# Hash-bucket attention and feed-forward in one kernel: work placed by step number instead of by generators, with reshaped hash loads

## Chip, cores, metric

The kernel runs on one core of a Trainium2 chip. The metric is the device time of one execution in microseconds (us). Kernels are compared through runs in the fast state, the quicker of two states.

The engines have short names here: PE does matmuls, ACT exps, DVE vector work, POOL copies and sums, and SP issues most of the DMA transfers. PSUM is the memory that matmuls write to.

## The reference, cut to what matters

```python
# q, k, v: (4, 8, 768, 64); proj: (64, 6); all float32
q_bits = (einsum('bhsd,dk->bhsk', q, proj) > 0)        # 6 sign bits per row, k likewise
mask   = q_bucket[:, :, :, None] == k_bucket[:, :, None, :]
scores = where(mask, scale * q @ k.T, -1e9)
attn   = softmax(scores) @ v
x      = attn.transpose(0, 2, 1, 3).reshape(B, S, 512)
xn     = (x - mean) / sqrt(var + 1e-6) * g_ln
out    = x + relu(xn @ w_ch1) @ w_ch2                  # 512 -> 2048 -> 512
```

Attention needs all heads of a batch before that batch's layer norm and feed-forward can start.

## The kernel before

Work is cut into 8 units (a batch and half its heads), each of 24 steps. A step is a pair (head, block of 128 keys): two score matmuls, one exp on ACT of 128x768, six attention matmuls. There are 192 steps; exp number n marks the start of step n in this text. A unit must be prepared before its first step: q and k are loaded twice (once by rows for the scores, once in 32-row chunks for the hash), the hash product is taken on PE in float32, its signs are appended to the rows, and the whole is transposed by DMA.

```python
def load_pair(ap, b, u):                      # issued at the start of a unit, for the next one
    hn = prep.tile([P, 4, NS * D], F32, tag="hashnat", bufs=2, name="hashnat")
    src = ap[b, hs].rearrange("h (c t s) d -> c h t (s d)", c=4, t=32)
    for c in range(4):
        nc.sync.dma_start(out=hn[:, c, :], in_=src[c])      # slowest source dim: 4 heads
    ...
# the main loop
for i in range(n_steps + LAG):
    ...scores(i); attend(i - LAG)
    if last step of batch b: ffq.append([i + FF_DELAY, b, feed_forward(b, layer_norm(b))])
    if i % 2 == 0: drain(nxt, 1)              # one more piece of the next unit's preparation
    credit = min(credit + 5.3, 8.0)           # feed-forward: up to 5.3 matmuls a step
    while ffq and ffq[0][0] <= i and credit >= 1.0: ...
# [cut: rest of the kernel]
```

A batch's feed-forward is 224 matmuls: 128 of 384 columns (first layer) and 96 of 512 (second). Relus are on DVE, as is the layer norm, emitted whole after the last head of a batch.

## Time and profile before

| | value |
|---|---|
| time, median of the first 3 runs | 512.64 us (508.14 to 519.0) |
| PE, DVE, ACT busy | 68%, 45%, 34% of the span |
| DMA queue of SP | 54.5% of 16 engines |
| exp 0 / 24 / 48 begin | 38.0 / 90.3 / 133.9 us |
| last exp begins / end of the span | 440.7 / 508.7 us |

The page's second part cuts the span in 40 slices; each digit is a busy share in tenths, and PEclk is the granted clock of PE in tenths. These rows are of the kernel before:

```profile
PE   0122339376926699689655896789368999909997
ACT  1001318254823145345612443446123555400000
PEclk9999855555558589899957999999677999968999
DMA  3965969759739334693469316934594110112101
```

PE does little for the first third. DMA is busier then, but the next view tells how. It is the busy time in stretches of 2 us (from, to, length; per engine busy time and count; then granted clock, DMA share, GB/s), kernel before:

```profile
12.00:14.00 2.00, 0.00 (x0) 0.00 (x0) 0.00 (x0) 0.00 (x0) 0.00 (x0) 1.00 0.27 100
...
46.00:48.00 2.00, 0.00 (x0) 0.00 (x0) 0.64 (x1) 0.00 (x0) 0.00 (x0) 1.00 0.27 99
...
76.00:78.00 2.00, 2.00 (x18) 1.28 (x17) 0.51 (x1) 1.86 (x3) 0.00 (x0) 0.50 0.98 406
```

Where hash loads run, the DMA share stands at about a quarter and 99 to 100 GB/s pass; where weights run, nearly all engines work and 406 GB/s pass. A share that stands still at a quarter says that 4 of 16 engines carry the transfer. That agrees with the Trainium skill, "DMA: Bandwidth & Descriptors", in the section on why a DMA adds 16 to its semaphore ("How many engines (k)"): the number of engines must divide the slowest dimension of both sides, and the source's slowest dimension is 4 heads.

The chain that ended last, in order of time (start, length, what), kernel before, shows such loads on the path in the middle too:

```profile
196.81 10.14 DMA hashnat<-in_k_dram
...
207.08 1.78 DVE hashT L116
...
211.33 1.51 PE hp L123 x16
```

A load issued at 196.81 us lands 10.14 us later, DVE transposes it, and the hash product follows on PE. Between 171 us and the last layer norm PE has six stops of over 2.5 us, of 3.2 to 8.3 us each.

### The profile page before, as it was taken

How to read it: one execution, taken by the hardware profiler on the slowest of the kernel's cores; microseconds unless marked ns; L12 is line 12 of the kernel's file. 1: busy time of each engine (PE TensorE's matmuls, PEld its weight loads, DVE VectorE, ACT ScalarE, POOL GpSimd, SP SyncE). 2: the span in 40 equal slices, each digit the busy share in tenths (PEclk: the TensorE clock that was granted, in tenths of full speed). 3: DMA queues.
4: the chain of work that ended last, by engine and by line, in shares of the span. 5: the costliest groups of instructions: out<-in, count | busy, mean ns of one | idle time of the engine just before them, and what ended most of it. 6: DMA issues, size and time to landing. Idle time of an engine off the chain costs nothing.

```text
span 508.7 us, 6653 instructions
## 1 busy us (share of the span) xinstructions
PE 344.2 (68%) x2696; PEld 191.4 (38%) x2696; DVE 229.6 (45%) x471; ACT 172.6 (34%) x193; POOL 67.5 (13%) x66
## 2 busy tenths in 40 slices
PE   0122339376926699689655896789368999909997
PEld 0011216243613255345423453455134556504453
DVE  0131054435492442463764424645744346385271
ACT  1001318254823145345612443446123555400000
POOL 3141140013110400150012201310104000000000
PEclk9999855555558589899957999999677999968999
DMA  3965969759739334693469316934594110112101
GB/s 102 187 149 141 294 166 283 258 152 170 151 89 178 80 63 109 187 140 84 132 146 191 70 51 185 193 71 118 122 195 107 40 41 1 43 26 59 41 22 62
DMA packets 90352, 62.31 MB, mean 122 GB/s; under 512 B 64209, under 2 KB 84689, under 8 KB 89809
## 3 DMA queue, kind: packets, MB, share of 16 engines
q1 hardware_dynamic: 90320, 61.88, 54.5%
q8 instruction: 21, 0.34, 0.3%
q14 instruction: 11, 0.08, 0.0%
HBM read 39.85 MB, written 6.29 MB: 91 GB/s over the span
## 4 chain that ended last, share of the span: by engine, by line
PE 37%; DMA 26%; DVE 21%; SPq 7%; issue 5%; POOL 2%; DVEq 0%; POOLq 0%
DMA hashnat<-in_q_dram 7%; PE sc L286 6%; DMA vnat<-in_v_dram 5%; SPq L99 4%; DMA hashnat<-in_k_dram 4%; DMA w1st<-in_moe_w_ch_dram 4%; PE av L303 3%; DVE hbuf L252 3%; DVE hashT L116 3%; DVE stats L200 3%; DMA scorenat<-in_k_dram 3%; DVE x L321 2%; PE hp L123 2%; DVE nd L315 2%; DVE xn L226 2%
## 5 line engine op out<-in xcount | busy, mean ns | idle before, releaser
L292 ACT ACTIVATE expb<-sc,bias_sb 128x768 bf16<-128x768 f32 x192 | 171.3, 902 | 268.0 <-PE sc L286 264.9
L286 PE MATMUL sc<-opT 70*128 70x384 bf16 x384 | 116.4, 392 | 4.9 <-DMA opT<-pad_86 1.7
L303 PEld LDWEIGHTS <-expb 128*128 128x128 bf16 x1152 | 73.5, 111 | 47.7 <-issue 30.5
L123 PE MATMUL hp<-hashT,projT 128*32 128x192 f32 x256 | 22.8, 503 | 88.2 <-DVE hashT L116 69.5
L247 PEld LDWEIGHTS <-w_sb 128*128 128x128 bf16 x512 | 48.6, 104 | 88.6 <-issue 56.2
L116 DVE STREAM_TRANSPOSE hashT<-hashnat 128x1536 f32<-128x1536 f32 x16 | 28.4, 1774 | 64.2 <-DMA hashnat<-in_k_dram 35.7
L286 PEld LDWEIGHTS <-opT 70*128 70x128 bf16 x384 | 37.9, 110 | 47.1 <-issue 27.2
L257 PEld LDWEIGHTS <-hbuf 128*128 128x128 bf16 x384 | 34.0, 97 | 32.4 <-issue 0.2
L123 PEld LDWEIGHTS hp<-hashT,projT 128*32 128x32 f32 x256 | 9.2, 153 | 94.3 <-DVE hashT L116 87.5
L303 PE MATMUL av<-vaug_92,expb 128*128 128x65 bf16 x432 | 30.0, 214 | 7.9 <-DVE nd L315 7.9
L303 PE MATMUL av<-vaug_91,expb 128*128 128x65 bf16 x432 | 29.5, 211 | 0.4 <-DVE nd L315 0.4
L315 DVE TENSOR_TENSOR nd<-av,vd 128x390 f32<-128x390 f32 x32 | 17.7, 553 | 23.4 <-PE av L303 23.4
L321 DVE TENSOR_TENSOR x<-nd,rec 128x384 f32<-128x384 f32 x32 | 21.9, 685 | 1.1
L112 POOL CAST pad_86<-scorenat 128x1536 bf16<-128x1536 f32 x5 | 7.5, 1490 | 110.4 <-DMA scorenat<-in_k_dram 69.4
L112 POOL CAST pad_85<-scorenat 128x1536 bf16<-128x1536 f32 x6 | 8.8, 1467 | 95.8 <-DMA scorenat<-in_k_dram 58.3
L112 POOL CAST pad_87<-scorenat 128x1536 bf16<-128x1536 f32 x5 | 7.3, 1468 | 106.1 <-DMA scorenat<-in_k_dram 78.7
L303 PE MATMUL av<-vaug_93,expb 128*128 128x65 bf16 x288 | 18.9, 207 | 0.0
L184 DVE TENSOR_SCALAR w_sb<-w1st,g_sb 128x2048 bf16<-128x2048 f32 x4 | 6.1, 1517 | 22.4 <-DMA w1st<-in_moe_w_ch_dram 22.4
L200 DVE BATCH_NORM_STATS2 stats<-x 128x6 f32<-128x512 f32 x24 | 16.0, 666 | 0.1
L226 DVE TENSOR_SCALAR xn<-x,mv,y 128x512 bf16<-128x512 f32 x24 | 11.3, 540 | 0.1
L247 PE MATMUL h_4072<-xT,w_sb 128*128 128x384 bf16 x4 | 1.5, 521 | 13.4 <-DMA xT<-xn 13.4
L189 DVE CAST w_sb<-w2st 128x2048 bf16<-128x2048 f32 x4 | 4.9, 1226 | 10.9 <-DMA w2st<-in_moe_w_ch_dram 10.9
(364 smaller groups left out, 401.1 us busy)
## 6 DMA issues: line engine op xcount, KB each, us to landing
hashnat<-in_k_dram SPq DMA_DIRECT2D x32, 192.0 KB
scorenat<-in_k_dram SPq DMA_DIRECT2D x8, 768.0 KB
hashnat<-in_q_dram SPq DMA_DIRECT2D x32, 192.0 KB
scorenat<-in_q_dram SPq DMA_DIRECT2D x8, 768.0 KB
vnat<-in_v_dram SPq DMA_DIRECT2D x8, 768.0 KB
out_dram<-res SPq DMA_DIRECT2D x24, 256.0 KB
w1st<-in_moe_w_ch_dram SPq DMA_DIRECT2D x4, 1024.0 KB
w2st<-in_moe_w_ch_dram SPq DMA_DIRECT2D x4, 1024.0 KB
```

What stands on the lines that cost most here:

```text
L112: nc.gpsimd.tensor_copy(pad[:, :, 0:D], sn.rearrange("p h (s d) -> p (h s) d", d=D))
L116: nc.vector.transpose(hT.rearrange("p c s j t -> p (c s j t)"), hn.rearrange("p c n -> p (c n)"))
L123: nc.tensor.matmul(hp[c * 32 : (c + 1) * 32, 0 : NS * 32], projT[:, j, :], hT[:, c, :, j, :], start=(j == 0), stop=(j == 1),)
L200: nc.vector.bn_stats(stats[:, s, :], x[:, s, :])
L226: nc.vector.tensor_scalar(xn[:, i, :], x[:, s, :], scalar1=mv[:, s, 0:1], scalar2=y[:, s : s + 1], op0=AOP.subtract, op1=AOP.mult,)
L247: nc.tensor.matmul(hp[:, 0:QH], w1_sb[:, o, n * P : (n + 1) * P], xT[hf][:, :, o, :], start=(o == 0), stop=(o == ND - 1),)
L257: nc.tensor.matmul(o2, hb[:, n, i * P : (i + 1) * P], w2_sb[:, n, :], start=(n == 0), stop=(n == NH - 1),)
L286: nc.tensor.matmul(sc[:, f, 0:QH], kT[0:KB, h * NS + t, :], qT[0:KB, h * NS + f * HALF : h * NS + (f + 1) * HALF, :],)
L292: nc.scalar.activation(e, sc[:, :, 0:QH], AF.Exp, scale=scale, bias=bias_sb)
L303: nc.tensor.matmul(av[:, s * VA : (s + 1) * VA], e[:, s // HALF, (s % HALF) * P : (s % HALF + 1) * P], va[:, h, t, :], start=(t == 0 and s ...
L315: nc.vector.tensor_add(nd, av[:, 0 : NS * VA].rearrange("p (s n) -> p s n", n=VA), vd[:, h : h + 1, :].to_broadcast([P, NS, VA]),)
L321: nc.vector.tensor_mul(xs[b][:, :, hd * D : (hd + 1) * D], nd[:, :, 0:D], rec.to_broadcast([P, NS, D]),)
```

## The change

The generators give way to a table from step number to actions. The stated intent: loads a unit ahead, stores and transposes issued late (when their data are ready), one hash transfer per head, the layer norm in pieces, and relus on two engines. The core of the diff, with cuts marked:

```diff
-        src = ap[b, hs].rearrange("h (c t s) d -> c h t (s d)", c=4, t=32)
-        for c in range(4):
-            nc.sync.dma_start(out=hn[:, c, :], in_=src[c])
+        src = ap[b, u * UH : (u + 1) * UH].rearrange("h (c t s) d -> h t c (s d)", c=4, t=32)
+        for h in range(UH):
+            eng.dma_start(out=hn[h * 32 : (h + 1) * 32], in_=src[h])
 ... (cut)
+    def plan_unit(n):
+        z = (n - 1) * UNIT
+        at(z + 0, cast_rows, n, "k")
+        at(z + 0, hash_turn, n, "k")
+        at(z + 3, hash_mm, n, "k")
+        at(z + 5, turn, n, "k")
 ...     (q likewise at 6, 6, 9, 11; v at 9 and 15)
+        if n + 1 < B * NU:
+            at(z + 3, load_hash, k, n + 1, "k", nc.sync)      # a unit ahead of its use
 ... (cut)
+                if n % 2:
+                    nc.scalar.activation(hb[:, n, :], hp[:, 0:QH], AF.Relu)
+                else:
+                    nc.vector.tensor_scalar_max(hb[:, n, :], hp[:, 0:QH], 0.0)
 ... (cut)
-                res = work.tile([P, DM], F32, tag="res", bufs=3, name="res")
-                nc.vector.tensor_add(res, o2, x[:, s, :])
-                nc.sync.dma_start(out=out_v[:, s, :], in_=res)
+                nc.vector.tensor_add(x[:, s, :], o2, x[:, s, :])
+                at(now[0] + 1, store, b, s)
 ... (cut: statistics of heads 0-3, 4-6 and 7 taken apart; x in 3 buffers, nd in 1)
+        first[b] = z + BATCH + FF_DELAY        # step 56, 104, 152, 200
+        if i < n_steps:
+            target = 0.0
+            for b in range(B):
+                left = TAIL_MM if b == B - 2 else 0                       # TAIL_MM = 45
+                span = BATCH if b < B - 2 else n_steps - first[b]
+                target += (N_FF - left) * min(max((i + 1 - first[b]) / span, 0.0), 1.0)
+        else:
+            target = done + 7
+        while ffq and done < target: ...
```

The first unit's q loads are also issued from ACT instead of SP, the tiny projection from the POOL queue, and the first unit is transposed in 4 parts.

More of the change, by code (lines that the diff above doesn't have):

```diff
@@ L69 @@
     for h in range(UH):
-        nc.sync.dma_start(
+        nc.gpsimd.dma_start(
             out=projT[h * 32 : (h + 1) * 32, :, h * NB : (h + 1) * NB], in_=proj_v
@@ L88, with at, run_step, load_hash @@
     w2ap = moe_w_ch2.rearrange("(o p) d -> p o d", p=P)
-    pad_no = [0]
+    todo = {}
+    def at(i, fn, *args):
+        todo.setdefault(i, deque()).append((fn, args))
+    def run_step(i):
+        for fn, args in todo.pop(i, ()):
+            fn(*args)
+    UNIT = UH * NS
     unit = {}
-    def load_pair(ap, b, u):
-        hs = slice(u * UH, (u + 1) * UH)
+    loaded = {}
+    half_done = {}
+    def load_hash(ap, n, key, eng):
+        b, u = divmod(n, NU)
         hn = prep.tile([P, 4, NS * D], F32, tag="hashnat", bufs=2, name="hashnat")
-        src = ap[b, hs].rearrange("h (c t s) d -> c h t (s d)", c=4, t=32)
-        for c in range(4):
-            nc.sync.dma_start(out=hn[:, c, :], in_=src[c])
+        src = ap[b, u * UH : (u + 1) * UH].rearrange("h (c t s) d -> h t c (s d)", c=4, t=32)
+        for h in range(UH):
+            eng.dma_start(out=hn[h * 32 : (h + 1) * 32], in_=src[h])
+        loaded[(n, key, "hash")] = hn
@@ L100, in load_pair, with load_rows @@
+    def load_rows(ap, n, key, eng):
+        b, u = divmod(n, NU)
         sn = prep.tile([P, UH, NS * D], F32, tag="scorenat", bufs=3, name="scorenat")
-        nc.sync.dma_start(
-            out=sn, in_=ap[b, hs].rearrange("h (p s) d -> p h (s d)", s=NS)
-        )
-        return hn, sn
-    def prep_side(ap, b, u, key):
-        hn, sn = load_pair(ap, b, u)
-        pad = pads[pad_no[0] % 3]
-        pad_no[0] += 1
-        yield
+        eng.dma_start(
+            out=sn,
+            in_=ap[b, u * UH : (u + 1) * UH].rearrange("h (p s) d -> p h (s d)", s=NS),
+        )
+        loaded[(n, key, "rows")] = sn
@@ L112, in prep_side, with pad_of, cast_rows, hash_turn @@
+    def pad_of(n, key):
+        return pads[(2 * n + (key == "q")) % 3]
+    def cast_rows(n, key):
+        sn = loaded.pop((n, key, "rows"))
         nc.gpsimd.tensor_copy(
-            pad[:, :, 0:D], sn.rearrange("p h (s d) -> p (h s) d", d=D)
+            pad_of(n, key)[:, :, 0:D], sn.rearrange("p h (s d) -> p (h s) d", d=D)
         )
+    def hash_turn(n, key):
+        hn = loaded.pop((n, key, "hash"))
         hT = prep.tile([P, 4, NS, 2, 32], F32, tag="hashT", bufs=1, name="hashT")
-        nc.vector.transpose(
-            hT.rearrange("p c s j t -> p (c s j t)"), hn.rearrange("p c n -> p (c n)")
-        )
@@ L119, in prep_side, with hash_mm @@
-        yield
+        for i in range(2):
+            nc.vector.transpose(
+                hT[:, 2 * i : 2 * i + 2].rearrange("p c s j t -> p (c s j t)"),
+                hn[:, 2 * i : 2 * i + 2].rearrange("p c n -> p (c n)"),
+            )
+        half_done[(n, key)] = hT
+    def hash_mm(n, key):
+        hT = half_done.pop((n, key))
         hp = ps_mm.tile([P, 512], F32, tag="mm", name="hp")
@@ L128, in prep_side @@
                 )
-        yield
         bits = prep.tile([P, NS, 32], F32, tag="bits", bufs=2, name="bits")
         nc.vector.transpose(bits.rearrange("p s n -> p (s n)"), hp[:, 0 : NS * 32])
-        dst = pad.rearrange("p (h s) n -> p h s n", s=NS)[:, :, :, D:KB]
+        dst = pad_of(n, key).rearrange("p (h s) n -> p h s n", s=NS)[:, :, :, D:KB]
         src = bits[:, :, 0 : UH * NB].rearrange("p s (h n) -> p h s n", n=NB)
@@ L138, in prep_side, with turn, value_cast, value_sum @@
             nc.vector.tensor_scalar_mul(dst, dst, 4.0 * BIG)
+    def turn(n, key, parts=1):
         tT = prep.tile([P, SL, P], BF16, tag="opT", bufs=4, name="opT")
-        nc.sync.dma_start_transpose(out=tT, in_=pad.rearrange("p a n -> p (a n)"))
-        unit[(b, u, key)] = tT
-        yield
-    def prep_v(b, u):
-        hs = slice(u * UH, (u + 1) * UH)
-        vn = prep.tile([P, UH, NS, D], F32, tag="scorenat", bufs=3, name="vnat")
-        nc.sync.dma_start(
-            out=vn.rearrange("p h s d -> p h (s d)"),
-            in_=v[b, hs].rearrange("h (p s) d -> p h (s d)", s=NS),
-        )
-        yield
-        va = vaugs[(b * NU + u) % 3]
+        w = SL // parts
+        for i in range(parts):
+            nc.sync.dma_start_transpose(
+                out=tT[:, i * w : (i + 1) * w, :],
+                in_=pad_of(n, key)[:, i * w : (i + 1) * w, :].rearrange("p a n -> p (a n)"),
+            )
+        unit[(n, key)] = tT
+    def value_cast(n):
+        vn = loaded.pop((n, "v", "rows")).rearrange("p h (s d) -> p h s d", d=D)
+        va = vaugs[n % 3]
         nc.gpsimd.tensor_copy(va[:, :, :, 0:D], vn)
-        v3 = prep.tile([P, UH, 3, D], F32, tag="v3", bufs=1, name="v3")
-        nc.gpsimd.tensor_add(v3, vn[:, :, 0:3, :], vn[:, :, 3:6, :])
         vs = prep.tile([P, UH, VA], BF16, tag="vs", bufs=1, name="vs")
         nc.gpsimd.memset(vs[:, :, D:VA], float(NS))
-        v1 = prep.tile([P, UH, D], F32, tag="v1", bufs=1, name="v1")
-        nc.gpsimd.tensor_add(v1, v3[:, :, 0, :], v3[:, :, 1, :])
-        nc.gpsimd.tensor_add(vs[:, :, 0:D], v1, v3[:, :, 2, :])
-        yield
+        nc.gpsimd.tensor_add(vn[:, :, 0:3, :], vn[:, :, 0:3, :], vn[:, :, 3:6, :])
+        nc.gpsimd.tensor_add(vn[:, :, 0, :], vn[:, :, 0, :], vn[:, :, 1, :])
+        nc.gpsimd.tensor_add(vs[:, :, 0:D], vn[:, :, 0, :], vn[:, :, 2, :])
+        half_done[(n, "v")] = (va, vs)
+    def value_sum(n):
+        va, vs = half_done.pop((n, "v"))
         vp = ps_mm.tile([P, 512], F32, tag="mm", name="vp")
@@ L165, in prep_v @@
         nc.vector.tensor_copy(vd.rearrange("p h n -> p (h n)"), vp[:, 0 : UH * VA])
-        unit[(b, u, "v")] = (va, vd)
-        yield
-    def prep_unit(b, u):
-        gens = [prep_side(k, b, u, "k"), prep_side(q, b, u, "q"), prep_v(b, u)]
-        for g in gens:
-            next(g)
-            yield
-        for g in gens:
-            for _ in g:
-                yield
-    def load_weights():
-        nc.sync.dma_start(out=g_sb, in_=moe_g_ln.rearrange("(o p) -> p o", p=P))
-        for o in range(ND):
-            st = work.tile([P, HID], F32, tag="hbuf", bufs=2, name="w1st")
-            nc.sync.dma_start(out=st, in_=w1ap[:, o, :])
-            yield
-            nc.vector.tensor_scalar_mul(w1_sb[:, o, :], st, g_sb[:, o : o + 1])
-        for o in range(4):
-            st = work.tile([P, 4, DM], F32, tag="hbuf", bufs=2, name="w2st")
-            nc.sync.dma_start(out=st, in_=w2ap[:, o * 4 : (o + 1) * 4, :])
-            yield
-            nc.vector.tensor_copy(w2_sb[:, o * 4 : (o + 1) * 4, :], st)
-        yield
@@ L193 @@
-    xs = {}
-    def layer_norm(b):
-        x = xs[b]
-        stats = work.tile([P, NS, 6], F32, tag="stats", bufs=2, name="stats")
+        unit[(n, "v")] = (va, vd)
+    def plan_unit(n):
[4 more added lines that the diff above has]
+        at(z + 5, turn, n, "k")
+        at(z + 6, cast_rows, n, "q")
+        at(z + 6, hash_turn, n, "q")
+        at(z + 9, hash_mm, n, "q")
+        at(z + 9, value_cast, n)
+        at(z + 11, turn, n, "q")
+        at(z + 15, value_sum, n)
+        if n + 1 < B * NU:
+            at(z + 3, load_hash, k, n + 1, "k", nc.sync)
+            at(z + 3, load_rows, k, n + 1, "k", nc.sync)
+            at(z + 9, load_hash, q, n + 1, "q", nc.sync)
+            at(z + 9, load_rows, q, n + 1, "q", nc.sync)
+            at(z + 15, load_rows, v, n + 1, "v", nc.sync)
@@ new lines, with load_w1, fold_w1, load_w2 @@
+    staged = {}
+    def load_w1(o):
+        st = work.tile([P, HID], F32, tag="hbuf", bufs=2, name="w1st")
+        nc.sync.dma_start(out=st, in_=w1ap[:, o, :])
+        staged[o] = st
+    def fold_w1(o):
+        nc.vector.tensor_scalar_mul(w1_sb[:, o, :], staged.pop(o), g_sb[:, o : o + 1])
+    def load_w2(o):
+        st = work.tile([P, 4, DM], F32, tag="hbuf", bufs=2, name="w2st")
+        nc.sync.dma_start(out=st, in_=w2ap[:, o * 4 : (o + 1) * 4, :])
+        staged[o] = st
+    def cast_w2(o):
+        nc.vector.tensor_copy(w2_sb[:, o * 4 : (o + 1) * 4, :], staged.pop(o))
@@ L198, in layer_norm, with stat, rstd @@
+    xs = {}
+    norm = {}
+    def stat(b, s, part, c0, c1):
+        if (s, part) == (0, 0):
+            norm[b] = work.tile([P, NS, 3, 6], F32, tag="stats", bufs=2, name="stats")
+        nc.vector.bn_stats(norm[b][:, s, part, :], xs[b][:, s, c0:c1])
+    def rstd(b):
+        stats = norm[b]
         mv = work.tile([P, NS, 2], F32, tag="mv", bufs=2, name="mv")
         for s in range(NS):
-            nc.vector.bn_stats(stats[:, s, :], x[:, s, :])
-            nc.vector.bn_aggr(mv[:, s, :], stats[:, s, :])
+            nc.vector.bn_stats(stats[:, s, 2, :], xs[b][:, s, DM - D : DM])
+        for s in range(NS):
+            nc.vector.bn_aggr(mv[:, s, :], stats[:, s, :, :].rearrange("p c n -> p (c n)"))
@@ L220, in layer_norm, with normalize, turn_x, store @@
             nc.vector.tensor_mul(y, y, t)
-        xT = []
-        for hf in range(2):
-            xn = work.tile([P, HALF, DM], BF16, tag="xn", bufs=2, name="xn")
-            for i in range(HALF):
-                s = hf * HALF + i
-                nc.vector.tensor_scalar(
-                    xn[:, i, :], x[:, s, :], scalar1=mv[:, s, 0:1],
-                    scalar2=y[:, s : s + 1], op0=AOP.subtract, op1=AOP.mult,
-                )
-            t_ = work.tile([P, HALF, ND, P], BF16, tag="xT", bufs=3, name="xT")
-            nc.sync.dma_start_transpose(
-                out=t_.rearrange("p s o n -> p (s o) n"),
-                in_=xn.rearrange("p s d -> p (s d)"),
-            )
-            xT.append(t_)
-        return xT
-    def feed_forward(b, xT):
-        x = xs[b]
-        out_v = out[b].rearrange("(p s) d -> p s d", s=NS)
-        for hf in range(2):
+        norm[b] = (mv, y)
+    xns = {}
+    def normalize(b, hf):
+        mv, y = norm[b]
+        xn = work.tile([P, HALF, DM], BF16, tag="xn", bufs=2, name="xn")
+        for i in range(HALF):
+            s = hf * HALF + i
+            nc.vector.tensor_scalar(
+                xn[:, i, :], xs[b][:, s, :], scalar1=mv[:, s, 0:1],
+                scalar2=y[:, s : s + 1], op0=AOP.subtract, op1=AOP.mult,
+            )
+        xns[(b, hf)] = xn
+    def turn_x(b, hf):
+        xn = xns.pop((b, hf))
+        t_ = work.tile([P, HALF, ND, P], BF16, tag="xT", bufs=3, name="xT")
+        nc.sync.dma_start_transpose(
+            out=t_.rearrange("p s o n -> p (s o) n"),
+            in_=xn.rearrange("p s d -> p (s d)"),
+        )
+        xns[(b, hf, "T")] = t_
+    now = [0]
+    def store(b, s):
+        out_v = out[b].rearrange("(p s) d -> p s d", s=NS)
+        nc.sync.dma_start(out=out_v[:, s, :], in_=xs[b][:, s, :])
+    def feed_forward(b):
+        x = xs[b]
+        for hf in range(2):
+            xT = xns.pop((b, hf, "T"))
             hb = work.tile([P, NH, QH], BF16, tag="hbuf", bufs=2, name="hbuf")
@@ L248, in feed_forward @@
                         hp[:, 0:QH], w1_sb[:, o, n * P : (n + 1) * P],
-                        xT[hf][:, :, o, :], start=(o == 0), stop=(o == ND - 1),
+                        xT[:, :, o, :], start=(o == 0), stop=(o == ND - 1),
                     )
-                    yield
-                nc.vector.tensor_scalar_max(hb[:, n, :], hp[:, 0:QH], 0.0)
+                    if o < ND - 1:
+                        yield
+                if n % 2:
+                    nc.scalar.activation(hb[:, n, :], hp[:, 0:QH], AF.Relu)
+                else:
+                    nc.vector.tensor_scalar_max(hb[:, n, :], hp[:, 0:QH], 0.0)
+                yield
             for i in range(HALF):
@@ L262, in feed_forward @@
                         yield
-                res = work.tile([P, DM], F32, tag="res", bufs=3, name="res")
-                nc.vector.tensor_add(res, o2, x[:, s, :])
-                nc.sync.dma_start(out=out_v[:, s, :], in_=res)
+                nc.vector.tensor_add(x[:, s, :], o2, x[:, s, :])
+                at(now[0] + 1, store, b, s)
                 yield
     LAG = 2
-    FF_DELAY = 8
+    FF_DELAY = 7
     N_FF = 2 * (NH * ND + HALF * NH)
+    BATCH = NU * UNIT
     steps = [
@@ L274 @@
     ]
-    UNIT = UH * NS
     exps = {}
     avs = {}
-    ffq = deque()
-    side = deque()
     def scores(i):
         b, u, h, t = steps[i]
-        qT, kT = unit[(b, u, "q")], unit[(b, u, "k")]
+        n = b * NU + u
+        qT, kT = unit[(n, "q")], unit[(n, "k")]
         sc = ps_sc.tile([P, 2, 512], F32, tag="sc", name="sc")
@@ L296, in attend @@
         b, u, h, t = steps[i]
-        va, vd = unit[(b, u, "v")]
+        va, vd = unit[(b * NU + u, "v")]
         if t == 0:
@@ L311, in attend @@
             if h == 0 and u == 0:
-                xs[b] = work.tile([P, NS, DM], F32, tag="x", bufs=2, name="x")
+                xs[b] = work.tile([P, NS, DM], F32, tag="x", bufs=3, name="x")
             hd = u * UH + h
-            nd = work.tile([P, NS, VA], F32, tag="nd", bufs=2, name="nd")
+            nd = work.tile([P, NS, VA], F32, tag="nd", bufs=1, name="nd")
             nc.vector.tensor_add(
@@ L324, in attend @@
             )
-    def drain(g, n=None):
-        c = 0
-        while n is None or c < n:
-            try:
-                next(g)
+    load_hash(k, 0, "k", nc.sync)
+    load_hash(q, 0, "q", nc.scalar)
+    load_rows(k, 0, "k", nc.sync)
+    load_rows(q, 0, "q", nc.scalar)
+    load_rows(v, 0, "v", nc.sync)
+    for key in ("k", "q"):
+        cast_rows(0, key)
+        hash_turn(0, key)
+        hash_mm(0, key)
+        if key == "k":
+            load_hash(k, 1, "k", nc.sync)
+        turn(0, key, UH)
@@ new lines @@
+    value_cast(0)
+    load_rows(k, 1, "k", nc.sync)
+    load_hash(q, 1, "q", nc.sync)
+    load_rows(q, 1, "q", nc.sync)
+    value_sum(0)
+    nc.sync.dma_start(out=g_sb, in_=moe_g_ln.rearrange("(o p) -> p o", p=P))
+    load_w1(0)
+    load_w1(1)
+    load_rows(v, 1, "v", nc.sync)
+    for n in range(1, B * NU):
+        plan_unit(n)
+    for o in range(4):
+        at(8 + 5 * o, fold_w1, o)
+        at(28 + 5 * o, cast_w2, o)
+        if o < 2:
+            at(8 + 5 * o, load_w1, o + 2)
+            at(28 + 5 * o, load_w2, o + 2)
+        else:
+            at(8 + 5 * o, load_w2, o - 2)
@@ new lines @@
+    first = {}
+    for b in range(B):
+        z = b * BATCH + LAG - 1
+        for s in range(NS):
+            at(z + UNIT + 2 * s, stat, b, s, 0, 0, UH * D)
+        for s in range(NS):
+            at(z + BATCH - NS + s, stat, b, s, 1, UH * D, DM - D)
+        at(z + BATCH, rstd, b)
+        at(z + BATCH, normalize, b, 0)
+        at(z + BATCH + 1, turn_x, b, 0)
+        at(z + BATCH + 1, normalize, b, 1)
+        at(z + BATCH + 3, turn_x, b, 1)
+        first[b] = z + BATCH + FF_DELAY
+    n_steps = len(steps)
@@ new lines @@
+    TAIL_MM = 45
+    ffq = deque()
+    done = 0
+    i = 0
+    while i < n_steps + LAG + FF_DELAY + 1 or ffq or any(j >= i for j in todo):
+        now[0] = i
+        if i < n_steps:
+            scores(i)
+        if LAG <= i < n_steps + LAG:
+            attend(i - LAG)
+        run_step(i)
+        for b in range(B):
+            if first[b] == i:
+                ffq.append(feed_forward(b))
+        if i < n_steps:
+            target = 0.0
+            for b in range(B):
+                left = TAIL_MM if b == B - 2 else 0
+                span = BATCH if b < B - 2 else n_steps - first[b]
+                target += (N_FF - left) * min(max((i + 1 - first[b]) / span, 0.0), 1.0)
+        else:
+            target = done + 7
+        while ffq and done < target:
+            try:
+                next(ffq[0])
+                done += 1
@@ L331, in drain @@
             except StopIteration:
-                return c
-            c += 1
-        return c
-    for _ in prep_unit(0, 0):
-        pass
-    nxt = prep_unit(0, 1)
-    drain(nxt, 3)
-    wts = load_weights()
-    credit = 0.0
-    n_steps = len(steps)
-    for i in range(n_steps + LAG):
-        if i < n_steps:
-            b, u, h, t = steps[i]
-            r = i % UNIT
-            if i and r == 0:
-                drain(nxt)
-                n = i // UNIT + 1
-                nxt = prep_unit(n // NU, n % NU) if n < B * NU else iter(())
-            scores(i)
-        if i >= LAG:
-            attend(i - LAG)
-            b, u, h, t = steps[i - LAG]
-            if (u, h, t) == (NU - 1, UH - 1, NS - 1):
-                ffq.append([i + FF_DELAY, b, feed_forward(b, layer_norm(b))])
-        if i < UNIT and i % 2 == 1:
-            drain(wts, 1)
-        if i % 2 == 0:
-            drain(nxt, 1)
-        credit = min(credit + 5.3, 8.0)
-        while ffq and ffq[0][0] <= i and credit >= 1.0:
-            if drain(ffq[0][2], 1) == 0:
@@ L364 @@
                 ffq.popleft()
-                continue
-            credit -= 1.0
-    while ffq:
-        drain(ffq.popleft()[2])
+        i += 1
 _INS = ['q', 'k', 'v', 'proj', 'moe_g_ln', 'moe_w_ch1', 'moe_w_ch2']
```

## The prediction

> **What bounds it now.** Nothing evenly; three stages. (Busy shares on the page: PE 68%, DVE 45%, ACT 34%; DMA 54.5% of 16 engines.)
>
> 1. 0 to 171 us, before any feed-forward: the load stream. First scores at 37.1 us (timeline), step 24 at 90, step 48 at 134 (counted exps), though a step needs ACT only 0.96 us. In stretches of 2 us the DMA share sits at exactly 0.27 with 99 GB/s wherever hash loads run (12-16, 26-28, 44-50, 104-110 us), while weights reach 341-406 GB/s. That is 4 of 16 engines. It agrees with the Trainium skill, "DMA: Bandwidth & Descriptors", section on the semaphore increment of 16, "How many engines (k)": k divides the slowest dim of both patterns, and the old source leads with 4 heads. The new pattern leads with 32 rows, so k should be 16. The old 786 KB takes about 7.9 us; I estimate 3.5-4 new.
> 2. 171 to 445 us: PE, broken by about one stop of 10-13 us per unit. The chain of waits shows load-issue, hash-load landing (10.1, 12.4, 10.2, 11.9 us), transpose 1.78, hash matmul. The loads are issued behind stores and transposes on SP, just before the in-order PE needs them. Layer norm also blocks DVE for about 12 us per batch.
> 3. 445 to 509 us: layer norm and transpose leave PE idle 13.4 us, then 50 us of feed-forward.
>
> **What changes.** Same matmuls and bytes. Loads come a unit (24 steps) ahead, so hash stops (about 12 us each) should vanish after start. Stores and transposes are issued when their data are ready, so SP no longer blocks (it waits 131.7 us at stores now). Half of the relus (0.56 us on DVE) go to ACT, estimated 0.55 us each there, 64 in all. One table load (1.28 us) should remain: "ScalarE: Activation LUTs", table sets, puts relu in every set; no trace of before tests it. Layer norm after the last head shrinks from about 11 to 7.5 us before the first transpose, and 45 matmuls (about 9 us) are held to cover it.
>
> **Sum (estimates from those durations).**
> - First scores at about 30 us instead of 37.
> - Steps 0-48 stay DMA-bound: loads of units 1, 2 and most of 3, 8.4 MB of weights (21 us), four transposes (3.75 each) make about 73 us, plus small gaps: step 48 at about 107.
> - First layer norm is not hidden (about 5 us of PE idle): feed-forward starts at about 121 instead of 171.
> - 136 steps with 627 feed-forward matmuls: at full clock a step's attention costs PE 0.44 us (1.325 us step less 5.3 matmuls of 0.163) and a feed-forward matmul 0.163 or 0.217: 60 + 117, plus ten hash products of 1.5, plus about 18 for PSUM waits on relu (DVE busy, ACT about 1.28 us a step in the first-layer phases, slightly over PE's 1.2): about 210 instead of 274.
> - Tail after the last step about 60 instead of 64.
>
> Predicted 392 us, 80% range 366 to 424. Chances: faster by over 2% 0.97, within 2% 0.02, slower 0.01.
>
> **Right or wrong shows as:** no long 0.27 DMA shares, hash loads near 200 GB/s; no PE wait over 3 us on the hash transpose after 121 us; PE busy 85-95% at clock near 1 from 121 us to the end; one table load; relu on ACT 0.5-0.6 us; PE idle in the final layer norm under 5 us instead of 13.4.
>
> **What would make it wrong:** hash loads into only 32 partitions at a time stay slow; transposes queued behind prefetched loads land late and scores wait at unit starts; weight folding on in-order DVE stalls attention in the first 48 steps; ACT's relus waiting on PE delay exps, making a PE-ACT lockstep; DVE (about 50 us of work per 63 us batch) becomes the limit.

## The result, and the profile after

The changed kernel takes 458.62 us (457.78 to 460.27, 4 runs), the kernel before 513.42 us. The ratio is 0.8967, with a 95% interval of 0.889 to 0.9044. Here and below, a ratio is from fast runs of the same rounds; it is not quite the ratio of the medians quoted, which are over all runs. The direction was right. The gain was 55 us where 121 was expected, and the time lies 35 us above the upper end of the range. All outputs are right.

The same rows of the changed kernel's page (40 slices of 11.4 us each):

```profile
PE   0476247936499998856899998864999988449996
ACT  1065144844230329966112169952303199503020
PEclk9998555785799999996699999977999999759999
DMA  8999999995493017990961068965110130030101
```

The first third is denser on DMA, as hoped. But look at ACT and PE together after the first third: where PE is at 9, ACT is mostly at 0 to 3; where ACT is at 9, PE is at 8. Attention and feed-forward alternate. In the kernel before, ACT stood mostly at 3 to 6 under a busy PE.

Busy time of two stretches of the changed kernel (columns as before: PE, weight loads, DVE, ACT, POOL, clock, DMA share, GB/s):

```profile
123.00:169.00 46.00, 45.76 (x240) 22.74 (x244) 13.64 (x24) 8.32 (x17) 2.93 (x2) 0.97 0.44 115
169.00:205.00 36.00, 27.86 (x359) 18.13 (x352) 21.90 (x46) 30.92 (x40) 7.92 (x7) 0.99 0.96 201
```

In the first stretch PE runs 240 matmuls, a whole feed-forward, and almost no attention. In the second ACT is busy for 30.92 of 36 us and PE for 27.86. The ACT timeline of the first stretch shows no exp before 168.54 us, and a hole of 11.62 us while PE runs the second layer:

```profile
134.01 0.49 ACT L312 ACTIVATE hbuf<-h_1176 128x384 bf16<-128x384 f32 x1 [0.97 <-PE h_1176 L305]
135.47 0.49 ACT L312 ACTIVATE hbuf<-h_1188 128x384 bf16<-128x384 f32 x1 [0.97 <-PE h_1188 L305]
147.58 0.49 ACT L312 ACTIVATE hbuf<-h_1255 128x384 bf16<-128x384 f32 x1 [11.62 <-PE h_1255 L305]
```

Why this is so can be read from the diff. For the last batch first[b] is 200 and n_steps is 192, so span is -8. At every step below 199 the fraction (i + 1 - 200) / -8 is positive, and it is clipped to 1 up to step 191. The last batch therefore adds 224 to the target from the first step on, although its feed-forward is not there yet. Each feed-forward is "behind" by a whole batch as soon as it may start, and is emitted in one block. The same excess uses up the 45 matmuls that were to be held for the last layer norm.

The starts of chosen exps, read from each trace (us); "first ff" is the first feed-forward matmul:

| kernel | exp 0 | 24 | 48 | 56 | first ff | 96 | 104 | 144 | 191 | end |
|---|---|---|---|---|---|---|---|---|---|---|
| before | 38.0 | 90.3 | 133.9 | 141.7 | 153.6 | 242.2 | 250.9 | 348.0 | 440.7 | 508.7 |
| changed | 25.5 | 70.7 | 106.9 | 115.5 | 122.1 | 204.9 | 213.7 | 302.8 | 394.0 | 457.5 |
| e1_pace | 25.5 | 70.2 | 106.3 | 114.9 | 121.4 | 182.4 | 201.3 | 260.2 | 332.8 | 397.7 |
| e2_hash | 26.3 | 69.5 | 103.5 | 111.2 | 121.9 | 199.4 | 208.2 | 298.2 | 385.1 | 453.2 |
| e3_oldhash | 43.9 | 100.7 | 148.7 | 157.4 | 163.3 | 255.0 | 263.6 | 360.4 | 452.7 | 515.2 |
| e5_pace_oldhash | 42.7 | 99.8 | 148.1 | 156.5 | 162.7 | 235.0 | 257.6 | 325.7 | 400.3 | 465.3 |
| e6_pace_sameunit | 25.4 | 60.3 | 93.7 | 101.4 | 108.9 | 169.3 | 181.4 | 243.7 | 317.7 | 383.5 |
| e10_sameunit_oldpace | 25.6 | 60.2 | 95.6 | 103.4 | 110.8 | 178.5 | 186.4 | 263.2 | 345.1 | 408.5 |

Up to step 56 the changed kernel runs as predicted (step 48 at 106.9 us, predicted about 107; first feed-forward at 122, predicted about 121). The error lies after it.

### The profile page after: what moved, and what is told of

It is laid out like the page before. It is cut to its first block, busy times and chain, and to the rows that moved or that the text cites. A ratio compares the mean times of both kernels' runs of the same rounds, so it can differ in the third digit from the quotient of the medians.

```text
span 457.5 us, 6762 instructions
## 1 busy us (share of the span) xinstructions
PE 345.7 (76%) x2688; PEld 190.4 (42%) x2696; DVE 202.7 (44%) x471; ACT 190.2 (42%) x257; POOL 71.0 (16%) x70
## 4 chain that ended last, share of the span: by engine, by line
PE 46%; DMA 21%; ACT 14%; DVE 9%; issue 4%; SPq 3%; POOL 1%; ACTq 0%; DVEq 0%
ACT expb L353 14%; DMA scorenat<-in_q_dram 4%; PE sc L347 3%; DMA scorenat<-in_k_dram 3%; DMA xT<-xn 3%; DMA opT<-pad_86 2%; DMA w1st<-in_moe_w_ch_dram 2%; DMA opT<-pad_85 2%; DMA opT<-pad_87 2%; PE hp L147 2%; SPq L167 2%; PE av L364 1%; DVE xn L275 1%; DMA hashnat<-in_q_dram 1%; DVE t L261 1%
## 5 line engine op out<-in xcount | busy, mean ns | idle before, releaser
L353 ACT ACTIVATE expb<-sc,bias_sb 128x768 bf16<-128x768 f32 x192 | 157.5, 921 | 106.4 <-PE sc L347 104.5
L347 PE MATMUL sc<-opT 70*128 70x384 bf16 x384 | 106.0, 361 | 45.4 <-DMA opT<-pad_85 11.4
L305 PEld LDWEIGHTS <-w_sb 128*128 128x128 bf16 x512 | 52.5, 103 | 78.2 <-issue 51.3
L364 PEld LDWEIGHTS <-expb 128*128 128x128 bf16 x1152 | 67.6, 105 | 33.4 <-issue 12.2
L347 PEld LDWEIGHTS <-opT 70*128 70x128 bf16 x384 | 35.2, 103 | 80.0 <-issue 79.2
L320 PEld LDWEIGHTS <-hbuf 128*128 128x128 bf16 x384 | 37.6, 98 | 45.7 <-issue 1.8
L136 DVE STREAM_TRANSPOSE hashT<-hashnat 128x768 f32<-128x768 f32 x32 | 29.2, 951 | 14.7 <-DMA hashnat<-in_k_dram 9.3
L364 PE MATMUL av<-vaug_91,expb 128*128 128x65 bf16 x432 | 28.1, 206 | 0.0
L364 PE MATMUL av<-vaug_92,expb 128*128 128x65 bf16 x432 | 27.5, 203 | 0.6 <-ACT expb L353 0.4
L364 PE MATMUL av<-vaug_93,expb 128*128 128x65 bf16 x288 | 17.4, 198 | 0.0
L238 DVE BATCH_NORM_STATS2 stats<-x 128x6 f32<-128x256 f32 (+1 forms) x48 | 16.1, 379 | 0.2
L179 POOL TENSOR_TENSOR scorenat<-scorenat 128x768 f32<-128x768 f32 x8 | 15.2, 1895 | 0.2
(345 smaller groups left out, 383.5 us busy)
```

The source lines that it names most:

```text
L136: nc.vector.transpose(hT[:, 2 * i : 2 * i + 2].rearrange("p c s j t -> p (c s j t)"), hn[:, 2 * i : 2 * i + 2].rearrange("p c n -> p (c n)"),)
L179: nc.gpsimd.tensor_add(vn[:, :, 0:3, :], vn[:, :, 0:3, :], vn[:, :, 3:6, :])
L238: nc.vector.bn_stats(norm[b][:, s, part, :], xs[b][:, s, c0:c1])
L305: nc.tensor.matmul(hp[:, 0:QH], w1_sb[:, o, n * P : (n + 1) * P], xT[:, :, o, :], start=(o == 0), stop=(o == ND - 1),)
L320: nc.tensor.matmul(o2, hb[:, n, i * P : (i + 1) * P], w2_sb[:, n, :], start=(n == 0), stop=(n == NH - 1),)
L347: nc.tensor.matmul(sc[:, f, 0:QH], kT[0:KB, h * NS + t, :], qT[0:KB, h * NS + f * HALF : h * NS + (f + 1) * HALF, :],)
```

## The experiments

Two theories stood against each other for the missing time. **Pacing:** the feed-forwards come in blocks through the sum above. **Lockstep:** relus on ACT that wait for PE, and the load on DVE, slow a mixed stage, so spreading the work would not help. A second question was where the gain of 54 us had come from: the shape of the hash loads, or the loads issued a unit ahead.

The experiments fall into four groups of rounds on three chips; the median of the kernel before was 512.0 to 513.0 us in each, so times are also compared across groups. The granted clock is no rival cause: in the first group the kernel before took 511.3 us at a mean clock of 0.816 and 509.5 us at 0.919.

### e1_pace: only the sum mended

```diff
-            for b in range(B):
+            for b in range(B - 1):
                 left = TAIL_MM if b == B - 2 else 0
```

> The changed kernel with one number altered: the pacing sum leaves out the last batch, whose span is negative and so adds a whole batch (224) to the target from the first step. Pacing theory (each batch's feed-forward is emitted in one block of 44 us without attention, then 48 steps of attention run alone at ACT's pace of about 0.81 us): with the sum mended the blocks are spread, first-stage times stay (feed-forward starts at about 122 us), the stage up to the last step shrinks from 273 to about 210 us, the end idle falls from 12 to under 5 us; 392 us, between 378 and 410. Lockstep theory[...]: spreading puts relus between the exps and cannot help; over 430 us.

Measured: 403.97 us, ratio to before 0.7892 (0.7835 to 0.7948). This is 55 us below the changed kernel, whose ratio was 0.8967, from one edit in the loop's range. Exps 56 to 191 now take 217.9 us in place of 278.5. Pacing holds and lockstep falls, since the relus that had moved to ACT stayed there and now stand between the exps. The same edit also lets the 45 matmuls be held; e7 below, which holds none, is still 49 us under the changed kernel, so the spreading is most of it. A stretch in the middle of this kernel, same columns:

```profile
201.30:260.20 58.90, 57.93 (x557) 35.05 (x558) 32.22 (x67) 42.07 (x56) 15.82 (x14) 1.00 0.87 192
```

PE is busy for 57.93 of 58.90 us at the full clock, with ACT at 42.07 beside it. What blocking had cost is thus time in attention-only stretches, where ACT set the pace, and layer norms that nothing covered. The list of waits (who waited for whom: total us, times, longest) of the changed kernel has the latter for each of the four batches:

```profile
PE h_4108 L305 <- DMA xT<-xn: 11.7, 1, 11.7
...
PE h_1098 L305 <- DMA xT<-xn: 6.6, 1, 6.6
PE h_3233 L305 <- DMA xT<-xn: 6.3, 1, 6.3
...
PE h_2169 L305 <- DMA xT<-xn: 5.4, 1, 5.4
```

In e1 one such wait is left, of 6.5 us, at the first batch, where there is no earlier feed-forward to run; three waits of 4.2 us for a PSUM bank stand beside the other layer norms.

### e2_hash: the kernel before with only the hash loads reshaped

```diff
-        src = ap[b, hs].rearrange("h (c t s) d -> c h t (s d)", c=4, t=32)
-        for c in range(4):
-            nc.sync.dma_start(out=hn[:, c, :], in_=src[c])
+        src = ap[b, hs].rearrange("h (c t s) d -> h t c (s d)", c=4, t=32)
+        for h in range(UH):
+            nc.sync.dma_start(out=hn[h * 32 : (h + 1) * 32], in_=src[h])
```

> The kernel before with only the hash loads reshaped: one transfer per head into 32 partitions with the row leading in both patterns, in place of one per chunk with the 4 heads leading. Engine-count theory (4 engines at 99 GB/s become 16 at about 215 GB/s): no stretches at a DMA share of 0.27, first scores at about 28 us instead of 37, each stop shorter by 5 to 8 us; 455 us, between 440 and 480. Issue-order theory (the stops come from issuing late behind stores and transposes on SP, whatever the width): 495 us or more.

Measured: 457.2 us, ratio 0.8922 (0.8858 to 0.8986). These three lines alone give what the whole change gave. First scores come at 25.5 us (expected about 28), and the still quarter share is gone. Of the 56 us, 32 are won before the first feed-forward and 25 between exps 56 and 191 (table above). Hash loads of the changed kernel, which have the same shape, look like this at its start (2 us stretch), then a stretch in which the rows for the scores are loaded, and one of weights:

```profile
8.00:10.00 2.00, 0.00 (x0) 0.00 (x0) 0.00 (x0) 0.00 (x0) 0.00 (x0) 1.00 1.10 215
...
12.00:14.00 2.00, 1.76 (x14) 0.56 (x12) 0.41 (x2) 0.00 (x0) 0.33 (x1) 1.00 1.06 373
...
38.00:40.00 2.00, 2.00 (x16) 0.84 (x15) 1.22 (x4) 0.00 (x0) 0.14 (x1) 0.50 1.00 404
```

215 GB/s is twice the old rate, though with all engines busy it is only half the rate of weights. (Shares a little above 1 occur in such short stretches; they are read as full.) The packets of both kinds of load are 1536 bytes in the trace: 279 of them at about 122 ns each from 8 to 10 us, where hash loads write 32 partitions, and 485 at about 70 ns from 12 to 14 us, where the rows are written to 128 partitions at 373 GB/s. So the length of the rows does not set 215 GB/s. The old hash loads, from the same source rows to 128 partitions, had packets of about 66 ns; what remains, though not tried alone, is the 32 partitions.

PE still waits for the hash transpose 57.8 us in e2, but mostly no longer for loads. DVE's idle time before the transposes that waited for hash loads (what ended it: us in all, times) in the kernel before was

```profile
  DMA hashnat<-in_k_dram: 35.7, 5
  DMA hashnat<-in_q_dram: 28.4, 5
```

and in e2

```profile
  DMA hashnat<-in_k_dram: 13.4, 2
...
  DMA hashnat<-in_q_dram: 1.6, 1
```

It fell from 64 to 15 us. One stop of PE that is left, from the timeline of e2:

```profile
199.95 1.86 SPq L99 DMA_DIRECT2D hashnat<-in_k_dram  x4
...
215.91 1.77 DVE L116 STREAM_TRANSPOSE hashT<-hashnat 128x1536 f32<-128x1536 f32 x1
217.28 3.58 SPq L99 DMA_DIRECT2D hashnat<-in_q_dram  x4
217.60 0.52 DVE L315 TENSOR_TENSOR nd<-av,vd 128x390 f32<-128x390 f32 x1
217.73 1.51 PE L123 MATMUL hp<-hashT,projT 128*32 128x192 f32 x16 [9.52 <-DVE hashT L116]
```

The load was issued at 199.95 us. The transpose has no idle time before it: DVE was in the layer norm until then, and PE waited 9.52 us behind that. A wait named after a load's consumer need not be a wait for the load.

### e3_oldhash and e5_pace_oldhash: hash loads back on 4 engines

The diff is that of e2 reversed, on the changed kernel (e3) and on the mended one (e5).

> The changed kernel with the hash loads put back to 4 engines. Engine-count theory: the load stream of the first stage is then bound by 4 engines, step 48 comes at about 135 us instead of 107, later loads mostly hide behind the feed-forward blocks: 485 us, between 475 and 505. If loading a unit ahead is what paid, it stays within 8 us of 459.

Measured for e3: 515.35 us, ratio 1.0061 (1.0004 to 1.0119), the same as before. All other parts of the change together are worth nothing in this state. It was slower than expected: step 48 came at 148.7 us, not 135, and exps 56 to 191 took 295.3 us in place of 278.5, so later loads did not all hide behind the feed-forward blocks.

> The paced version with hash loads on 4 engines. If the reshaped hash loads pay in the first stage only: first feed-forward at 163 us as in the unpaced run with 4 engines, against 121, and little after that: 450 us. If the 4 engines also bind later (4 hash loads of 7.9 us per batch beside everything else that those engines carry, an estimated 76 us per 78 us batch): 460 to 480 us. Over 420 us in any case.

Measured for e5: 467.13 us, ratio 0.915 (0.9119 to 0.9181). Against e1 the first feed-forward starts 41 us later (162.7 in place of 121.4), and the other 22 us come later on. So the 4 engines bind beyond the first stage too. Read together, the hash shape is worth 56 to 63 us wherever it was tried (before to e2: 56; e3 to changed: 57; e5 to e1: 63), and the mended sum 48 to 55 (e3 to e5, changed to e1).

### e4_pace_dverelu: all relus on DVE

```diff
-                if n % 2:
+                if False:
                     nc.scalar.activation(hb[:, n, :], hp[:, 0:QH], AF.Relu)
```

> The paced version with all relus on DVE. Prediction's view: PE waits for its two product banks in the first-layer phases; about 10 us slower than the paced version (5 to 20). Lockstep theory: faster than the paced version, as ACT is then free for exps.

Measured: 407.26 us, ratio 0.7922 (0.7855 to 0.799), against 0.7892 for e1 in the same rounds; the intervals overlap. Splitting the relus is worth at most about 3 us, which is not clear of the noise, not 10.

### e6_pace_sameunit: the mended kernel without loading ahead

```diff
-        at(z + 0, cast_rows, n, "k")      # of unit n; loads of unit n + 1 at z + 3, 9, 15
-        ...
+        at(z + 0, load_hash, k, n, "k", nc.sync)   # and rows; q at z + 2, v at z + 4
+        at(z + 6, cast_rows, n, "k")
+        at(z + 6, hash_turn, n, "k")
+        at(z + 8, hash_mm, n, "k")
+        at(z + 10, turn, n, "k")                   # q at z + 12, 14, 16; v at z + 16, 20
```

> The paced version with each unit's loads issued at the start of the unit in which they are prepared (steps 0, 2 and 4, preparation at steps 6 to 20, as in the kernel before), not a unit ahead. If loading a unit ahead is what removes the stops on the hash product: 30 to 50 us slower than the paced version, waits of PE for the hash transpose back at 8 us or more per unit. If hash loads on 16 engines (786 KB in about 4 us) come in time anyway and what remained were waits for DVE: within 8 us of the paced version.

Measured: 386.43 us, ratio 0.7536 (0.7473 to 0.7599). Neither theory had this: it is 17 us faster than e1. Loading a unit ahead, the first item of the stated intent, costs time. The issues on SP show how. In e1 (start, length, what):

```profile
34.01 5.58 SPq L111 DMA_DIRECT2D hashnat<-in_k_dram  x4
39.69 0.39 SPq L117 DMA_DIRECT2D scorenat<-in_k_dram  x1
41.93 12.29 SPq L167 DMA_TRANSPOSE opT<-pad  x1
...
54.90 2.05 SPq L111 DMA_DIRECT2D hashnat<-in_q_dram  x4
57.04 0.40 SPq L117 DMA_DIRECT2D scorenat<-in_q_dram  x1
57.54 9.54 SPq L167 DMA_TRANSPOSE opT<-pad  x1
```

and in e6:

```profile
34.05 12.92 SPq L167 DMA_TRANSPOSE opT<-pad  x1
...
47.69 6.16 SPq L167 DMA_TRANSPOSE opT<-pad  x1
```

The two transposes are those of unit 1, which step 24 needs. In e1 the loads of unit 2, not needed before step 48, stand in front of them; the second transpose is issued until 67.08 us instead of 53.85, and step 24 begins at 70.2 instead of 60.3. Unit 1 is prepared at the same steps in both kernels, so only the moved loads can be the cause there. (For later units the edit also moves the preparation; this was not taken apart.) Of the 17 us, 13.5 lie before step 56. The first stage is bound by the load stream, so whatever is fetched early delays what is due. PE's waits of scores for transposed q and k (us in all, times, longest) show it, e1 first and e6 below:

```profile
PE sc L347 <- DMA opT<-pad: 19.4, 3, 9.5
...
PE sc L358 <- DMA opT<-pad: 4.6, 2, 2.7
```

In the later stages the two are equal: exps 56 to 191 take 217.9 us in e1 and 216.3 in e6. With loads on 16 engines, fetching at the start of the unit is early enough.

### e7_pace_notail and e8_pace_wholeln: two smaller parts

e7 sets TAIL_MM to 0 in e1; e8 takes the layer-norm statistics whole after the last head in e1.

> The paced version that holds no feed-forward back for the last layer norm (45 becomes 0). Prediction's view: about 9 us of work was held to cover an idle of about 12; without it PE idles 12 us at the end in place of about 6, so 5 to 9 us slower.

Measured for e7: 409.78 us, ratio 0.8023 (0.7989 to 0.8058), 6 us over e1. The held matmuls pay as expected.

> The paced version with the layer-norm statistics taken whole after the last head, as in the kernel before, not in pieces. DVE's run before the first transpose grows by about 4 us per batch, which PE meets three times behind the hash product's bank and once at the end: 8 to 16 us slower. If the chain were hidden, under 4 us.

Measured for e8: 412.16 us, ratio 0.8077 (0.8041 to 0.8112), 8 us over e1, at the lower edge of what was expected.

### e9_pace_hashlater: what stops PE beside a layer norm

In e1, steps 96 to 104 and 144 to 152 take 19 us each, where e6 takes 12. The timeline of e1 at the first of them:

```profile
193.69 0.38 DVE L154 STREAM_TRANSPOSE bits<-hp 128x192 f32<-128x192 f32 x1
...
194.12 1.01 PE L320 MATMUL o<-w_sb,hbuf 128*128 128x512 bf16 x2 [4.17 <-DVE bits L154]
```

The hash product and the feed-forward share two banks of PSUM. The reader of the hash product stands on DVE behind the layer norm, and so a feed-forward matmul waits for a bank.

```diff
+        m = 5 if n % 2 and n > 1 else 0            # units that begin beside a layer norm
-        at(z + 3, hash_mm, n, "k")                 # and the transposes, q's product and loads after it
+        at(z + 3 + m, hash_mm, n, "k")
-        at(z + BATCH + 1, normalize, b, 1)
+        at(z + BATCH + 4, normalize, b, 1)
```

> The paced version (loads a unit ahead, 404 us) with the hash products of the units that begin beside a layer norm moved 5 steps later, and the second half of the normalize 3 steps later. If the 19 us that steps 96 to 104 and 144 to 152 take (in place of about 12) come from the hash product's bank, whose reader sits behind the layer norm on DVE: these stretches fall to about 13 us and the time to 392, between 386 and 398. If DVE's chain stops PE at some other matmul then: within 5 us of 404.

Measured: 397.0 us, ratio 0.775 (0.7693 to 0.7808), 7 us under e1. Steps 96 to 104 fall from 18.9 to 12.0 us, so the bank was what stopped PE there. The time is within the range but 5 us over the value expected: the 16 steps after them grow from 22.8 to 29.8 us, with a new PE wait of 4.81 us for the transposed q and k, whose preparation had moved too. At this batch nothing is won in all. The two kept traces do not locate the 7 us: exps 56 to 191 take 217.4 us in e9 and 217.9 in e1, and these two executions took 400.0 and 399.5 us.

### e10_sameunit_oldpace: the old pace in the best schedule

```diff
-            target = 0.0 ... (the mended sum)
+        credit = min(credit + 5.3, 8.0)
+        target = done + math.floor(credit)
```

> The paced version with loads in their own unit (386 us) with the feed-forward paced as in the kernel before: up to 5.3 matmuls a step until a batch is used up, nothing held for the end. If even pacing, which leaves PE feed-forward work to do during the layer norms, is what divides this family from the kernel before with new hash loads (457 us): 415 to 435 us, with PE busy under 75% in the windows around layer norm. If the rest of the schedule (stores and transposes when ready, pieces) is: 390 to 400 us.

Measured: 409.74 us, ratio 0.7996 (0.7948 to 0.8044), 23 us over e6 but 5 below the range of the pacing theory. The edit takes away two things, even pacing and the matmuls held for the end: at the last layer norm PE waits 10.4 us for the transposed x in e10, and in e6 no such wait shows. Even pacing leaves PE work to do during the layer norms: in e6, steps 96 to 104 beside one have PE busy for 11.99 of 12.10 us. In e10 a stretch around one (same columns as above) reads

```profile
185.00:205.00 20.00, 12.91 (x104) 7.13 (x104) 14.19 (x31) 7.57 (x11) 7.99 (x7) 0.74 1.05 203
```

PE is busy for 65% there.

### e11_best and e12_hash_evenpace

e11 is e6 with second-layer weights loaded after unit 2, the k hash products beside a layer norm 2 steps later, and the second half of normalize 8 steps later.

> The paced version with loads in their own unit, with second-layer weights loaded behind the third unit's rows, hash products beside a layer norm 2 steps later, and the second half of normalize and its transpose 8 and 7 steps later. Estimate: 5 us less in the first stage, about 2 us less at each layer norm: 376 us, between 368 and 386.

Measured: 393.97 us, ratio 0.7706 (0.765 to 0.7763). This is a miss: 7.5 us slower than e6. Step 56 came earlier (95.6 us in place of 101.4), but the first feed-forward did not (109.5 against 108.9), and exps 56 to 191 took 230 us in place of 216. In e11 PE waits 13.6 us for the first transposed x, at 109.5 us, so what the first stage won was lost there. The three edits were not taken apart.

e12 puts only the reshaped hash loads and the mended, even pace into the kernel before. Even pacing keeps three batches of x alive, so the parts of the change that save memory (residual and value sums in place, one nd buffer) are needed too.

> The kernel before with two parts of the change: the reshaped hash loads and an even feed-forward pace over 48 steps (the last of the three over the 39 steps left), with what this pace needs in memory (a third x buffer; residual and value sums in place; one nd buffer). Layer norm whole, relus on DVE, generator order as before. If even pacing is worth in this order what it is worth in the event schedule (23 us): 434 us, between 426 and 442, against 457 with the hash loads alone. If it needs the shorter layer norm or the other pieces to pay: 445 us or more; if it were all that divides 457 from 386: under 400.

Measured: 447.09 us, ratio 0.8715 (0.8627 to 0.8803), 10 us under e2. Even pacing, with what it needs in memory, is worth 10 us in the old order; in the new one it is worth 23 us together with the held matmuls. So it seems to need other pieces of the schedule to pay in full. That is not shown cleanly, as e12 holds nothing for the end and its first exp comes 4.8 us later than that of e2.

## Why the prediction was wrong

- **The step that failed** is "136 steps with 627 feed-forward matmuls: ... about 210 instead of 274". Counted as there, from the first feed-forward matmul to the last exp, it took 272 us in the changed kernel and 211 once the sum was mended (e1). So the sum of its costs was sound; its single terms were not checked. What was false is that these matmuls are spread over the steps: the pacing sum releases each batch in one block. The diff held the answer, since span is -8 for the last batch. The whole-kernel estimate of 392 us met 404 in the mended kernel, inside the stated range of 366 to 424. One sign named for being right could not tell the two apart: from the first feed-forward on PE was busy 85% of the time in the changed kernel (285 of 335 us, at a mean clock of 0.92), within the 85 to 95% foretold, and 93% in e1.
- **"45 matmuls are held to cover it"** failed for the same reason: nothing was left to hold, and PE's wait for the last transposed x was 11.7 us, not under 5. The prediction put the tail at 60 us; last exp to end is 63.5. In e1, where holding works, it was worth 6 us (e7).
- **The first stage was right, in part by luck.** The estimate of 4 engines and then 16 is confirmed by e2, e3 and e5, with hash loads at 215 GB/s. First scores came at 24.7 us (predicted 30), step 48 at 106.9 (107), first feed-forward at 122 (121). The hit on step 48 is two errors that cancel: the start was 5 us early, and steps 0 to 48 took 81 us instead of 77.
- **"Loads come a unit ahead, so hash stops should vanish"** was the wrong reason. After 121 us the changed kernel indeed has no PE wait over 2.5 us on the hash transpose, but neither has e6, which issues each unit's loads later. The wide loads removed most of DVE's waits for hash data by themselves (64 to 15 us in e2). Loading ahead then only cost: 17 us in e1 against e6. The warning that transposes could stand behind prefetched loads was on the list of what could go wrong, and it happened, hidden inside a first-stage sum that had simply counted those loads in.
- **The relu split** was costed well per instruction (ACT 0.49 us, estimated 0.55; one table load, as predicted), but it is worth at most about 3 us (e4). The lockstep that was feared does not appear.
- **Two readings of the kernel before were off.** The stage without feed-forward was said to end at 171 us, but the first feed-forward matmul ran at 153.6. And "one stop of 10-13 us per unit" took the landing times of loads for stops: PE's six stops after 171 us make 31.5 us together, and the two longest (8.3 us) stand behind the layer norm on DVE.
- **Still open:** between e2 (457) and e6 (386) lie 71 us. Even pacing and the held matmuls account for 23 (e6 to e10); by e7 some 6 of these may be the holding. The remaining 48 (e2 to e10) fall, by the two traces, 11 before the first feed-forward, 32 between exps 56 and 191 and 5 after the last exp. Which parts of the schedule they belong to is open: e8 and e4 show 8 and at most 3 in e1, which do not simply add, and the stores, halved hash transposes and event times were not tried alone.

The best version run is e6, at 386.43 us: the changed kernel with one loop range mended and each unit's loads issued in its own unit.

## What to carry to other kernels

Before costing a schedule, print the order it really emits: a pacing formula with a negative span looked harmless and cost 48 to 55 us, nearly what the best part of the change gained. When a DMA share stands still at a simple fraction, count the engines that the access pattern allows before moving the issue earlier. And prefetch only where the load stream has slack; in a stage that it bounds, fetching ahead of need delays what is due.

## What the Trainium skill lacked or had wrong

- "DMA: Bandwidth & Descriptors" ("How many engines (k)") was right and decisive: 4 heads leading gave a share of 0.27 and 99 GB/s, 32 rows leading a share of 1.10 and 215 GB/s.
- The same page, "Rules for kernel authors", says to issue a DMA early to overlap it with compute. It lacks the limit: in a stage bound by the load stream, issuing a unit ahead put the first feed-forward 12.5 us later (121.4 in e1, 108.9 in e6).
- "ScalarE: Activation LUTs", table sets, says relu is in every set; the trace agrees: 192 exps and 64 relus in turn, one table load of 1.28 us.
- The same page's rules say to put relu on VectorE, as per element faster in bf16. It gives no such comparison for a float32 source in PSUM: for 128x384, ACT took 0.49 us here and DVE 0.56, so the advice does not carry over to this shape.
